# The second pair's q and k are loaded ahead of the first weights, and two loads of weights wait for a word from VectorE

## The chip, the cores and the metric

The kernel runs on one core of a Trainium2 chip, as one program. The metric is the device time of one execution in microseconds (us). The kernel before was timed three times: 749.03 us median (748.67 to 751.96). One more execution was recorded by the hardware profiler and gives all rows below: it took 752.57 us, of which 750.9 us are the span of the trace and the other 1.7 us lie around it.

The engines are called as in the profile: PE is TensorE, DVE VectorE, ACT ScalarE, POOL GpSimd, and SP is SyncE, which does nothing here but issue transfers. Each engine works through its own instructions in order, and so does the queue of transfers that SP issues: an instruction that waits holds up all that stand behind it on that engine.

## The reference

Windowed attention with a linear bias, over 8 batches, 8 heads, 576 positions and a head size of 64, followed by a layer that takes the elementwise maximum of three products:

```
scores = q @ k.T / sqrt(64) + bias              # per batch and head
attn   = softmax(where(0 <= i - j < 128, scores, -1e9))
x      = (attn @ v), heads side by side         # 4608 x 512
h      = max(max(x @ w1, x @ w2), x @ w3)       # 4608 x 768
out    = h @ w_out                              # 4608 x 512
```

## The kernel before, in words

Two heads make a task, four tasks a batch. A task's queries are cut into blocks of 128, and one block of the two heads is a *step*; two tasks share their last half block, so that two tasks make nine steps. Two steps that follow each other are a *turn pair*: they share a set of statistics, and their probabilities are transposed together.

A step runs through four engines. `products` (line 431, PE) multiplies q and k of two steps into PSUM; these are the first users of a task's q and k. `score` (lines 447 to 461, DVE) moves the masked half over the other, adds the bias and takes the row maximum. `exps` (line 473, ACT) takes the exponential and its row sums. `sums_of` (line 479 on ACT, line 480 on DVE) makes the reciprocals of a pair, and `normalise` scales the probabilities with them, on POOL (line 487) or ACT (line 492). `turn` (line 500, PE) transposes the pair, ACT copies it out of PSUM (lines 504, 509, 512), POOL cuts the two triangles (lines 520 and 524), and `mix` (line 545, PE) multiplies with v. Products of a step that holds the last half block of one task and the first block of the next need q and k of both tasks. That happens first in the third pair of steps.

The twelve groups of weights are prepared beside this. `fetch` (line 152) loads one group of 1 MB, in a 64-bit form; `exponents` and `convert` (lines 166, 177, 186 on DVE for the first six groups, lines 170 and 171 on ACT later) make floats of it; `part` (lines 200 and 203) splits these into a high and a low part; lines 327 and 216 write them back to DRAM, as `plain` and `keep`. There are two buffers for raw groups (the tiles `hs`, two buffers under this name): a group can be fetched only when the one two ahead of it is done, its `plain` written included. `preparing` is this sequence for all groups, and each call of `weights(n)` lets it advance by n of its pieces.

What is issued when is set by `events`, a list of steps with times in units of a step, sorted and run at the end of the kernel: `score` of step s at s + 0.04, `exps` at s + 0.3, and so on; `weights` stands in it at 2.06, and from step 5 on at every s + 0.2. A scheduler may still move instructions past each other on an engine, except those marked `keep_in_program_order`, which hold their order among themselves: `score` of the steps below 4, and the transfers and spins that say so. `spin` puts products of zeros on PE between other work.

Ahead of the events stand the first loads, all on SP's queue: q and k of task 0 in two pieces, the first group of weights, q and k of task 1, v of task 0, the second group of weights. `load` and `load_v` are the transfers of a task's q and k and of its v, with two buffers each: the load for task 2 waits until PE is through with task 0.

After the first batch's steps PE starts on the products of the layer (line 767, then line 791), whose left operands are the split weights in `ring`, and from there on it goes through the batches with attention of the next one in between.

Of the kernel before, what the change touches and what calls it, by code (L numbers as in the profile page):

```python
# [8 lines left out]
F32 = mybir.dt.float32  # L9
# [28 lines left out]
def attention_maxout_kernel(  # L38
# [11 lines left out]
    nc = tc.nc  # L50
# [40 lines left out]
    for a in range(2):  # L91
        for d in (slice(0, P),) if a == 0 else (slice(0, D), slice(D, P)):
            nc.gpsimd.affine_select(
                out=prev[d, a], in_=prev[d, a], pattern=[[1, P]], compare_op=ALU.is_gt, fill=0.0,
# [13 lines left out]
    def slopes_t(pair):  # L108
        for h in range(2):
            d = slice(h * D, (h + 1) * D)  # L110
            for j in range(2):
                nc.gpsimd.tensor_scalar(  # L112
                    out=bias_t[d, pair, j], in0=dist[d, 1], scalar1=slope(4 * pair + 2 * h + j), scalar2=None,
                    op0=ALU.mult,
                )

    def slopes(hp):
        for h in (2 * hp, 2 * hp + 1):
            nc.scalar.activation(bias[:, h, :], dist[:, 0], AF.Copy, scale=slope(h))
        nc.gpsimd.affine_select(  # L120
            out=bias0[:, 2 * hp:2 * hp + 2], in_=bias[:, 2 * hp:2 * hp + 2], pattern=[[0, 2], [-1, P]],
            compare_op=ALU.is_ge, fill=-NEG, base=0, channel_multiplier=1,
        )
# [21 lines left out]
    SMALL = DM // 2  # L145

    def raw_tile():
        return hs_p.tile([P, SMALL + 4 * DM], I32, name="hs2", bufs=2)

    def fetch(g):  # L150
        r = raws[g] = raw_tile()
        nc.sync.dma_start(r[:, SMALL:].bitcast(U8)[:, :16 * DM - 3], w_all[g].bitcast(U8)[:, 3:])

    def pieces(g):
# [167 lines left out]
    def preparing():  # L322
        for n, g in enumerate(g_order):
            exponents(g, n < FEW)
            yield
            convert(g, n < FEW)
            nc.sync.dma_start(plain_keep[g], floats(g))
            yield
            for k in range(2):
                while g < 9 and not ahead(g, 1):  # L330
                    yield True
                part(g, k)
                if k == 1 and n + 2 < NG:
                    fetch(g_order[n + 2])
                yield
# [51 lines left out]
    qkt, vt = {}, {}  # L387


    def load(t):  # L390
        b, hp = tasks[t]
        qkt[t] = qk_p.tile([P, 2, S], F32, name="qk")
        for cs in (slice(0, 2 * P), slice(2 * P, S)) if t == 0 else (slice(0, S),):
            nc.sync.dma_start(qkt[t][:, :, cs], qk[b, hp, :, :, cs])

    def load_v(t):
        b, hp = tasks[t]
        vt[t] = v_p.tile([P, NB + 1, P], F32, name="v")
        nc.sync.dma_start(vt[t], v[b, hp])
# [38 lines left out]
    def score(s):  # L438
        t, i = steps[s]
        b, hp = tasks[t]  # L440
        ps, a = banks.pop(s)
        first = tc.keep_in_program_order if s < 4 else lambda x: x
        if i:
            mask = prev[:, i == NB].bitcast(mybir.dt.uint8)
            if a is None:
                for x in ps:
                    first(nc.vector.copy_predicated(x[:, P:2 * P], mask, x[:, :P]))
            else:
                both = scores[:, :, a * 2 * P:(a + 1) * 2 * P]
                first(nc.vector.copy_predicated(  # L450
                    both[:, :, P:], mask.unsqueeze(1).broadcast_to([P, 2, P]), both[:, :, :P],
                ))

        if s % 2 == 0:
            stats[s // 2] = st_p.tile([P, 3, 2, 2], F32, name="st")
        st = stats[s // 2]
        less[s] = []
        for j in range(2):
            x = s_p.tile([P, P], F32, name="s", bufs=3)
            below = bias_t[:, hp // 2, j] if i == NB else (bias if i else bias0)[:, 2 * hp + j, :]  # L460
            first(nc.vector.tensor_tensor_reduce(  # L461
                out=x, in0=ps[j][:, P:2 * P], in1=below,
                scale=-0.125, scalar=3.0e38, op0=ALU.add, op1=ALU.min, accum_out=st[:, 0, s % 2, j:j + 1],
            ))
            less[s].append(x)
# [406 lines left out]
    def at(when, what, *args):  # L872
        events.append((when, len(events), what, args))
# [3 lines left out]
    for s, (t, i) in enumerate(steps):  # L877
        c = s + shift[tasks[t][0]]
        if i == LOAD_I and t + 2 < len(tasks):
            at(c - 0.4, load, t + 2)  # L880
        if i == NB - 1 and t + 1 < len(tasks):
            at(c - 0.4, load_v, t + 1)
        if i == 0 and 0 < t < NP:
            at(c - 1, slopes, t)
            if t % 2 == 0:
                at(c - 1, slopes_t, t // 2)
        at(c + 0.04, score, s)
        at(c + 0.3, exps, s)
        if s % 2 == 0:
            at(c + 0.002, products, s)  # L890
            at(c + DRAIN[0].get(n_steps - s, LAG_T) + 0.003, turn, s)
        else:
            at(c + (0.6 if s == n_steps - 1 else 1.1), sums_of, s)
            at(c + (0.8 if s == n_steps - 1 else 1.5), normalise, s)
# [31 lines left out]
            when += pace if u < 77 * b + 63 else O_PACE  # L926
    for u in range(77 * B, 77 * B + 3):
        at(when, unit, u)
    at(2.06, weights, 1)
    for s in range(5, n_steps + 2):  # L930
        at(s + 0.2, weights, 1.4 if s > 5 else 0.6)
    for s in range(3, n_steps, 2):
# [7 lines left out]
    spin(FIRST_SPIN)  # L940
    load(0)
    nc.scalar.dma_start(dist[:, 2], c_ident)
    fetch(0)
    slopes(0)
    slopes_t(0)
    load(1)
    load_v(0)
    nc.scalar.copy(out=plus, in_=dist[:, 2])
    fetch(1)
    for _, _, what, args in sorted(events, key=lambda e: e[:2]):  # L950
        what(*args)

# [37 lines left out]
```

## Time and profile before

| | us |
|---|---|
| median of three runs | 749.03 |
| profiled execution | 752.57 |
| its span | 750.9 |
| PE busy | 733.9 (98%) |
| DVE busy | 515.2 (69%) |
| ACT busy | 487.2 (65%) |
| POOL busy | 236.4 (31%) |

The busy times are of the whole span. PE is busy for nearly all of it, but part of that in the first 57 us are the spins. What a change at the start is worth is read from the few waits of PE, from the granted clock of PE by stretches, and from the order of the first instructions in time. A row of the timeline gives the start, the duration, the engine, the line, the operation with its tiles, how many instructions are merged in the row, and in brackets the idle time ahead of it with what ended that.

### The profile page before, as it was taken

How to read it: one execution, taken by the hardware profiler on the slowest of the kernel's cores; microseconds unless marked ns; L12 is line 12 of the kernel's file. 1: busy time of each engine (PE TensorE's matmuls, PEld its weight loads, DVE VectorE, ACT ScalarE, POOL GpSimd, SP SyncE). 2: the span in 40 equal slices, each digit the busy share in tenths (PEclk: the TensorE clock that was granted, in tenths of full speed). 3: DMA queues.
4: the chain of work that ended last, by engine and by line, in shares of the span. 5: the costliest groups of instructions: out<-in, count | busy, mean ns of one | idle time of the engine just before them, and what ended most of it. 6: DMA issues, size and time to landing. Idle time of an engine off the chain costs nothing.

```text
span 750.9 us, 19281 instructions
## 1 busy us (share of the span) xinstructions
PE 733.9 (98%) x7209; PEld 674.6 (90%) x7214; DVE 515.2 (69%) x1614; ACT 487.2 (65%) x1603; POOL 236.4 (31%) x451
## 2 busy tenths in 40 slices
PE   7999989999999999999999999999999999999998
PEld 3459988999999999999999999999999999999998
DVE  4888887536659477784778567794777747683673
ACT  5786976766667767676677757776666767552342
POOL 4661224645556123212222123222222122343100
PEclk8999999999999999999999999999999999999999
DMA  7877999759998489855988378864988468899611
GB/s 252 274 282 298 330 340 331 253 187 340 361 349 275 134 279 303 273 181 192 322 294 276 116 266 304 291 213 146 330 289 273 163 228 272 252 291 355 230 61 64
DMA packets 57085, 192.81 MB, mean 257 GB/s; under 512 B 5792, under 2 KB 24480, under 8 KB 50464
## 3 DMA queue, kind: packets, MB, share of 16 engines
q0 software_dynamic: 20304, 108.54, 43.9%
q1 hardware_dynamic: 36400, 82.85, 31.2%
q8 instruction: 57, 0.93, 0.5%
q14 instruction: 36, 0.29, 0.1%
q10 hardware_dynamic: 288, 0.20, 0.1%
HBM read 156.95 MB, written 34.60 MB: 255 GB/s over the span
## 4 chain that ended last, share of the span: by engine, by line
PE 77%; DVE 11%; ACT 7%; DMA 2%; issue 1%; POOL 1%; SPq 0%; DVEq 0%; ACTq 0%; POOLq 0%
PE ps_m L846 46%; PE ps_m L791 16%; PE ps_s L431 5%; PE pt L500 4%; PE ps_x L567 4%; DVE hs L615 2%; DVE hq L733 2%; ACT p L473 2%; DVE t L732 2%; DMA qk<-in_qk 1%; PE ps_x L545 1%; DMA hs<-in_w_all 1%; ACT p L492 1%; DVE t L618 1%; DVE xs L615 1%
## 5 line engine op out<-in xcount | busy, mean ns | idle before, releaser
L846 PE MATMUL ps_m<-xs,ring 128*128 128x288 f32 x2160 | 302.7, 297 | 0.6
L846 PEld LDWEIGHTS ps_m<-xs,ring 128*128 128x128 f32 x2160 | 290.1, 188 | 3.7 <-ACT t L863 3.4
L520 POOL TENSOR_SCALAR_AFFINE_SELECT pp<-pr 128x256 f32<-128x256 f32 x112 | 53.9, 482 | 277.2 <-ACT pr L504 154.0
L473 ACT ACTIVATE p<-s,st 128x128 f32<-128x128 f32 x288 | 114.7, 400 | 20.8 <-DVE st L461 17.2
L863 ACT COPY t<-ps_m 128x288 f32<-128x288 f32 x196 | 76.7, 394 | 71.2 <-PE ps_m L846 69.5
L791 PE MATMUL ps_m<-xs,ring 128*128 128x288 f32 x846 | 118.1, 297 | 2.8 <-DVE hq L808 2.2
L791 PEld LDWEIGHTS ps_m<-xs,ring 128*128 128x128 f32 x846 | 113.3, 188 | 4.1 <-DVE hq L808 2.4
L367 POOL DMA_DIRECT2D ring<-keep x103 | 55.5, 539 | 165.5 <-PE ps_m L846 157.3
L846 PE MATMUL ps_m<-hs,ow 128*128 128x288 f32 x756 | 105.8, 297 | 0.4
L846 PEld LDWEIGHTS ps_m<-hs,ow 128*128 128x128 f32 x756 | 100.9, 188 | 2.6 <-ACT t L863 1.2
L492 ACT ACTIVATE p<-p,st 128x128 f32<-128x128 f32 x252 | 84.6, 393 | 24.1 <-DVE st L480 24.1
L732 DVE TENSOR_TENSOR t<-ps_m,t 128x288 f32<-128x288 f32 x108 | 48.8, 453 | 42.8 <-PE ps_m L846 32.5
L461 DVE CUSTOM_DVE_ANT_0 s<-ps_s,bias 128x128 f32<-128x128 f32 x240 | 60.6, 285 | 9.0 <-POOL bias_t L112 3.4
L431 PE MATMUL ps_s<-qk 64*64 64x192 f32 (+1 forms) x1088 | 62.0, 319 | 3.4 <-DMA qk<-in_qk 2.4
L614 ACT CAST hs<-hq 128x288 fp32r<-128x288 f32 x96 | 40.2, 432 | 30.8 <-DVE hq L733 18.1
L473 ACT ACTIVATION_READ_ACCUMULATOR p<-s,st 128x1 f32 x288 | 55.3, 192 | 0.0
L567 PE MATMUL ps_x<-pp,v 64*64 64x64 f32 (+3 forms) x1456 | 53.4, 274 | 0.1
L567 PEld LDWEIGHTS ps_x<-pp,v 64*64 64x64 f32 x1456 | 41.7, 133 | 10.5 <-issue 8.6
L500 PE MATMUL pt<-plus,p 128*128 128x128 f32 x288 | 48.5, 289 | 2.0 <-POOL p L487 1.3
L524 POOL TENSOR_SCALAR_AFFINE_SELECT pp<-pr 128x256 f32<-128x256 f32 (+1 forms) x112 | 50.0, 447 | 1.1
L733 DVE TENSOR_TENSOR hq<-t,hq 128x288 f32<-128x288 f32 x108 | 48.8, 457 | 2.1
L601 DVE TENSOR_TENSOR xk<-ps_x,xk 128x256 f32<-128x256 f32 (+3 forms) x56 | 25.4, 454 | 36.0 <-ACT xk L600 36.0
(94 smaller groups left out, 942.0 us busy)
## 6 DMA issues: line engine op xcount, KB each, us to landing
ring<-keep POOLq DMA_DIRECT2D x51, 1024.0 KB, 7.4
ring<-keep POOLq DMA_DIRECT2D x61, 768.0 KB, 6.1
qk<-in_qk SPq DMA_DIRECT2D x31, 576.0 KB, 5.3
hs<-in_w_all SPq DMA_DIRECT2D x12, 1023.6 KB, 7.2
v<-in_v SPq DMA_DIRECT2D x32, 320.0 KB, 6.5
outT<-t SPq DMA_DIRECT2D x64, 144.0 KB, 1.8
keep<-ring SPq DMA_DIRECT2D x9, 768.0 KB, 6.5
plain<-hs SPq DMA_DIRECT2D x12, 512.0 KB, 4.0
```

Source lines behind the costliest of these rows:

```text
L367: nc.gpsimd.dma_start(wts[n, a], keep[n % 9][a])
L431: pe(nc.tensor.matmul(ps[j][d:d + D, o:o + k1 - k0], lhsT=qkt[u][j * D:(j + 1) * D, 0, q0:q0 + D], rhs=qkt[u][j * D:(j + 1) * D, 1, k0:k1] ...
L461: first(nc.vector.tensor_tensor_reduce(out=x, in0=ps[j][:, P:2 * P], in1=below, scale=-0.125, scalar=3.0e38, op0=ALU.add, op1=ALU.min, acc ...
L473: nc.scalar.activation(p[:, j], x, AF.Exp, bias=st[:, 0, a, j:j + 1], scale=-1.0, accum_out=st[:, 1, a, j:j + 1])
L492: nc.scalar.activation(p[:, j], p[:, j], AF.Copy, scale=st[:, 2, a, j:j + 1])
L500: pe(nc.tensor.transpose(out=pt[:, a, j], in_=p[:, j], identity=ident))
L567: pe(nc.tensor.matmul(x[j * D:(j + 1) * D, r, o:o + rhs.shape[1]], lhsT=vv[k, i, j * D:(j + 1) * D], rhs=rhs[k], start=start, stop=True, s ...
L732: nc.vector.tensor_tensor(out=s, in0=ps, in1=e, op=ALU.add)
L733: nc.vector.tensor_tensor(out=h, in0=s, in1=h, op=ALU.max)
L791: pe(nc.tensor.matmul(ps, lhsT=lt, rhs=rt, start=n == 0 and not (b == 0 and v < EARLY), stop=n == len(pairs) - 1, skip_group_check=True,))
L846: pe(nc.tensor.matmul(part_of[n, {2: 0, 5: 0, 6: 0, 3: 1}.get(kk, kk)], lhsT=lt, rhs=rt, start=first, stop=i == len(pairs) - 1, skip_group ...
L863: nc.scalar.copy(out=e, in_=ps)
```

## The change

Three things are done.

- `load(1)`, q and k of the second task, is issued ahead of `fetch(0)`, the first group of weights.
- `fetch(0)` is held back: DVE copies one word of task 0's q and k into the buffer of the weights, and the transfer overwrites this word. So it can't be issued before the first piece of q and k has landed and DVE has copied the word.
- `fetch(1)` leaves the first loads and becomes an event at 4.07, where DVE first writes one zero to its buffer. The first piece of the weights' preparation, line 166 for group 0, moves from 2.06 to 4.06, just ahead. `score` of step 4 joins the instructions that keep their program order, so both stand behind that step's scores on DVE.

```
-    def fetch(g):
+    def fetch(g, behind=False):
         r = raws[g] = raw_tile()
+        if behind:
+            tc.keep_in_program_order(nc.vector.memset(r[:, SMALL:SMALL + 1], 0))
+        if g == 0:
+            tc.keep_in_program_order(nc.vector.tensor_copy(out=r[:, SMALL:SMALL + 1].bitcast(F32), in_=qkt[0][:, 0, :1]))
         nc.sync.dma_start(r[:, SMALL:].bitcast(U8)[:, :16 * DM - 3], w_all[g].bitcast(U8)[:, 3:])
...
-        first = tc.keep_in_program_order if s < 4 else lambda x: x
+        first = tc.keep_in_program_order if s < 5 else lambda x: x
...
-    at(2.06, weights, 1)
+    at(4.06, weights, 1)
+    at(4.07, fetch, 1, True)
...
     load(0)
     nc.scalar.dma_start(dist[:, 2], c_ident)
+    load(1)
     fetch(0)
     slopes(0)
     slopes_t(0)
-    load(1)
     load_v(0)
     nc.scalar.copy(out=plus, in_=dist[:, 2])
-    fetch(1)
```

The lines below line 150 move down by four in the kernel after, and by a few more further on (166 becomes 170, 461 becomes 465, 480 becomes 484). Names with a number are single buffers.

The first rows of SP's queue are these before: `qk` are q and k, `hs` the raw weights, and a load of 128x1152 is a whole task.

```order
L394 DMA qk<-in_qk 128x2x256
L394 DMA qk<-in_qk 128x2x320
L152 DMA hs_161<-in_w_all 128x8189
L394 DMA qk<-in_qk 128x1152
L399 DMA v<-in_v 128x640
L152 DMA hs_177<-in_w_all 128x8189
L394 DMA qk<-in_qk 128x1152
```

The same place of SP's queue after:

```order
L398 DMA qk<-in_qk 128x2x256
L398 DMA qk<-in_qk 128x2x320
L398 DMA qk<-in_qk 128x1152
L156 DMA hs_163<-in_w_all 128x8189
L403 DMA v<-in_v 128x640 x2
L398 DMA qk<-in_qk 128x1152
L156 DMA hs_277<-in_w_all 128x8189
```

The load of the second task has moved ahead of the first weights, and the second weights have moved behind the v of task 1 and the q and k of task 2.

On DVE the scores of the second pair of steps, the first piece of the weights (166) and the reciprocals of the first pair (480) stand like this before:

```order
L461 ISA s,st<-ps_m_206,bias 128x128
L461 ISA st 128x1
L166 TENSOR_SCALAR hs_161<-hs_161 128x1024
L480 RECIPROCAL st<-st 128x4
L447 COPY_PREDICATED ps_m_205<-prev,ps_m_205 128x128
```

After, DVE's stretch from the same scores on begins so:

```order
L465 ISA s,st<-ps_m_205,bias 128x128
L465 ISA st 128x1
L484 RECIPROCAL st<-st 128x4
L451 COPY_PREDICATED ps_m_204<-prev,ps_m_204 128x128
L451 COPY_PREDICATED ps_m_205<-prev,ps_m_205 128x128
```

and a few rows further on DVE (`bias_t` marks step 4) it has:

```order
L465 ISA s,st<-ps_s,bias_t 128x128
L465 ISA st 128x1
L170 TENSOR_SCALAR hs_163<-hs_163 128x1024
L153 MEMSET hs_277 128x1
L484 RECIPROCAL st<-st 128x4
```

The first pair's reciprocals no longer stand behind the weights, but the second pair's now do, and the zero that lets group 1 be fetched stands behind the first piece of group 0.

The scheduler's order changes later too. On SP, where the seventh group of weights is written back and the ninth is fetched, it is before:

```order
L327 DMA plain_140<-hs_708 128x1024
L216 DMA keep_0_124<-ring 128x512
L216 DMA keep_1_125<-ring 128x1536
L394 DMA qk<-in_qk 128x1152
L152 DMA hs_860<-in_w_all 128x8189
```

The same place on SP after:

```order
L331 DMA plain_140<-hs_710 128x1024
L220 DMA keep_0_124<-ring 128x512
L398 DMA qk<-in_qk 128x1152
L220 DMA keep_1_125<-ring 128x1536
L156 DMA hs_862<-in_w_all 128x8189
```

The write of 768 KB (`keep_1`) has moved behind the load of q and k, directly ahead of the fetch.

## Rows read from the trace of the kernel before

**Rows 1.** PE's waits above 2 us but the start: total, times, longest.

```profile
PE ps_s L431 <- DMA qk<-in_qk: 2.4, 1, 2.4
PE ps_m L791 <- DVE hq L808: 2.2, 1, 2.2
```

**Rows 2.** Windows of 0.5 and 2 us: length, PE busy, granted clock, DMA share, GB/s.

```profile
10.50:11.00 0.50, 0.00 (x0) 0.59 1.04 435
...
17.50:18.00 0.50, 0.50 (x5) 1.00 0.00 0
...
102.00:104.00 2.00, 0.00 (x0) 1.00 0.67 238
```

**Rows 3.** Timeline of the first 20 us, all engines.

```profile
4.27 1.35 PE L431 MATMUL ps_s<-qk 64*64 64x128 f32 x16
...
9.66 0.41 POOL L120 TENSOR_SCALAR_AFFINE_SELECT bias<-bias 128x256 bf16<-128x256 bf16 x1
9.79 0.83 DVE L166 TENSOR_SCALAR hs<-hs 128x1024 int8<-128x1024 int8 x1 [1.39 <-DMA hs<-in_w_all]
10.54 0.16 DVE L480 RECIPROCAL st<-st 128x4 f32<-128x4 f32 x1
...
10.79 0.61 POOL L487 TENSOR_TENSOR p<-p,st 128x256 f32<-128x256 f32 x1 [0.71 <-DVE st L480]
...
11.26 1.34 PE L431 MATMUL ps_s<-qk 64*64 64x192 f32 x14 [2.41 <-DMA qk<-in_qk]
...
12.53 1.11 PE L500 MATMUL pt<-plus,p 128*128 128x128 f32 x4
...
14.21 0.22 ACT L479 ACTIVATE st<-st 128x4 f32<-128x4 f32 x1
...
15.14 0.62 POOL L487 TENSOR_TENSOR p<-p,st 128x256 f32<-128x256 f32 x1
...
19.34 0.59 ACT L504 COPY pr<-pt 128x512 f32<-128x512 f32 x1 [2.58 <-PE pt L500]
```

**Rows 4.** The page's group for the exponentials on ACT.

```profile
L473 ACT ACTIVATE p<-s,st 128x128 f32<-128x128 f32 x288 | 114.7, 400 | 20.8 <-DVE st L461 17.2
```

**Rows 5.** Timeline from 20 to 30 us, all engines.

```profile
22.10 2.06 POOL L487 TENSOR_TENSOR p<-p,st 128x256 f32<-128x256 f32 x2
...
22.92 0.77 DVE L166 TENSOR_SCALAR hs<-hs 128x1024 int8<-128x1024 int8 x1
...
24.21 0.44 PE L500 MATMUL pt<-plus,p 128*128 128x128 f32 x2 [0.58 <-POOL p L487]
...
25.20 0.18 DVE L480 RECIPROCAL st<-st 128x4 f32<-128x4 f32 x1 [1.09 <-ACT st L479]
...
26.18 1.58 POOL L487 TENSOR_TENSOR p<-p,st 128x256 f32<-128x256 f32 x1
...
28.04 0.30 DVE L447 COPY_PREDICATED ps_m<-prev,ps_m 128x128 f32<-128x128 uint8 x1 [0.75 <-PE ps_m L431]
...
28.33 0.66 PE L500 MATMUL pt<-plus,p 128*128 128x128 f32 x4
```

**Rows 6.** PE's timeline at the first product of the layer.

```profile
57.52 2.67 PE L791 MATMUL ps_m<-xs,ring 128*128 128x288 f32 x18 [0.63 <-DVE xs L615]
```

**Rows 7.** Transfers issued from 3.6 to 4.2 us: size, us to landing.

```profile
hs<-in_w_all SPq DMA_DIRECT2D x1, 1023.6 KB, 10.7
```

**Rows 8.** Transfers issued from 26.4 to 26.8 us.

```profile
hs<-in_w_all SPq DMA_DIRECT2D x1, 1023.6 KB, 5.1
```

**Rows 9.** SP's issues from 62 to 80 us, start and duration.

```profile
66.65 1.28 SPq L216 DMA_DIRECT2D keep<-ring  x2
70.22 0.33 SPq L394 DMA_DIRECT2D qk<-in_qk  x1
```

**Rows 10.** A window of 1 us, columns as in rows 2.

```profile
68.00:69.00 1.00, 1.00 (x10) 1.00 1.02 397
```

**Rows 11.** The chain that ended last, from 0 to 130 us: start, us, what.

```profile
70.65 7.38 DMA hs<-in_w_all
```

## The prediction

> **What bounds the kernel now.** I read first the waits of PE over the whole span [rows 1], then the granted clock in short windows [rows 2], then the first 30 us in order of time [rows 3, 5]. The reader is to see that PE hardly waits: beside the start, which the change leaves alone, two waits are over 2 us. One of them, 2.4 us for q and k of task 1, belongs to the loads that the change reorders. The timeline places it: PE stops at 11.26 - 2.41 = 8.85 us and goes on at 11.26 [rows 3]. The windows show a second cost of it: the granted clock is down to a mean of 0.59 between 10.50 and 11.00, after some 2 us in which PE did nothing, and only from 17.50 on is it 1.00 again [rows 2]; in between PE ran at 1.2 GHz instead of 2.4. The timeline shows a third: DVE stood idle for 1.39 us, to 9.79, waiting for the first weights, and behind line 166 on DVE stood the reciprocals of the first pair (10.54), for which POOL waited 0.71 us [rows 3]. So the first 30 us are bound by a chain of small steps through all engines, not by PE's throughput, and what they lose goes straight into the end: PE starts its layer at 57.52 [rows 6], when the steps let it, and hardly waits from there on.
>
> **The change part by part.** I follow the first pairs of steps, with durations from the rows, and give for each point the time before and after.
>
> *First transposes.* DVE is through with the scores of the second step at 9.79 - 1.39 = 8.40, and line 480 now stands there, so the reciprocals come at about 8.5 instead of 10.54. POOL can't use that at once: it works on bias tables until 9.66 + 0.41 = 10.07 [rows 3]. Its scaling takes 0.61, so it ends at 10.68 and PE transposes from 10.7 instead of 12.53. Q and k of task 1 must be there by 8.85 for this. They now have 576 KB of task 0 and two small tables ahead of them, in place of these and 1 MB of weights; DMA moved about 400 GB/s when full [rows 10], so I put them at 7 to 7.5 us. PE's products then end by 9.6 at the latest (fourteen took 1.34 us at half clock), and PE has a new wait of about 1.1 us, for POOL.
>
> *Clock.* This wait is half the old one, and the clock fell only after some 2 us of nothing. I take it to stay at 1.00. If so, the four transposes take 0.66 as at 28.33 [rows 5] and not 1.11, and with one product that now stands among them they end at 11.5; before they ended at 13.64.
>
> *Second pair.* From the end of the transposes to the end of POOL's scaling of the second pair it took 15.14 + 0.62 - 13.64 = 2.12 us [rows 3], all of it copies on ACT and cuts on POOL, which the clock doesn't touch. So 13.6. Transposes of 0.66 end at 14.3. ACT has, behind line 479 (14.21 before, 0.57 after the transposes, so 12.1 now), six exponentials and scalings of about 0.4 each [rows 4], which ends at 14.5. I put the copy of line 504 at 14.7 instead of 19.34: 4.6 earlier.
>
> *Third pair.* From there to the transposes at 24.21 it took 4.87 us, cuts and scalings on POOL (22.10 to 24.16 the last) that nothing in the change shortens. So 19.6, still 4.6 earlier. DVE has more to do beside this than before: lines 166 and 177 of group 0, which it used to do while it waited anyway, now stand further back. The reciprocals at 25.20 had waited 1.09 us for ACT; in the new order ACT has one exponential and one copy more ahead of line 479 (about 0.65), so I put them at 21.1, 4.1 earlier. At 28.04 DVE had waited 0.75 for PE [rows 5]. With PE 4.6 and DVE 4.1 ahead I take **4.4 us** for this place.
>
> *The held weights.* The copied word costs DVE one tiny instruction at about 4.3, while DVE waits for the first scores anyway; cost nothing, and if that cover were gone a tenth of a us. SP stands still for it until about 4.5, since PE's first products show the first piece of q and k to be there at 4.27 [rows 3], and behind it stand only v of tasks 0 and 1, needed at about 13. Group 0, issued at 4.5, must land by 11.6 (line 166 needs 0.83, and the reciprocals behind it wait for ACT until 12.4). The zero for group 1 follows at about 11.9; before, group 1 was issued at 3.8 and used at 22.92 [rows 5]. With everything 4 us earlier it is due at about 19. One transfer of weights took 5.1 us in a quieter queue [rows 8] and 10.7 with two loads and the other weights ahead [rows 7]. I take 6, near the quieter row, since less than 1 MB is queued ahead of each: 10.5 and 17.9, both in time. At the other end (15.2 and 22.6, later still with the first) the 4.4 are lost.
>
> *Later.* Between 28 and 57 us PE waits for no transfer (the one for q and k is at 11 us, [rows 1]); I carry the 4.4 through. Then the new order on SP counts. The two writes left at 66.65, and the load of q and k at 70.22, when PE let go of a buffer [rows 9]; the fetch behind it lands after 7.38 us and stands in the chain that ended last [rows 11]. Now the second write, 768 KB, leaves behind the load and ahead of the fetch. At 397 GB/s [rows 10] it delays the fetch by up to 1.98 us; part of it is given back, since the old write was still running when the fetch started and since PE reaches the products that free the buffer somewhat sooner. Bounds 0 and 2.0; I take the middle, **1.0 us**. The chain goes from there to PE's wait for line 808 near 102 us [rows 1], so I let it through in full.
>
> The Trainium skill (DMA: Bandwidth & Descriptors, "Queues, rings and completion order") says that each DMA engine takes the descriptors of a queue in ring order. The order of landing bears it out: the first weights end DVE's wait at 9.79, and q and k, issued behind them, end PE's at 11.26 [rows 3]. By that rule alone the whole 768 KB would pass ahead of the fetch, and the sum would be 4.4 - 2.0 = 2.4.
>
> Sum: 4.4 - 1.0 = 3.4 us. The profiled execution would go from 752.57 to 749.2; it lies 3.5 above the median of the runs shown, and I take the same 3.4 from the median: 749.03 - 3.4 = **745.6 us**.
>
> **The rivals.**
> - *The front's gain arrives whole.* If the moved write costs nothing, or the new order on ACT (each pair's exponentials a little earlier against the weights) shortens the wait of 2.2 at 102 us, the gain is 4.4 to 6.6: 742.4 to 744.6. For it: PE's waits there come from one chain that a reorder can relieve. Against it: the rows on DVE ahead of that wait stand nearly as before. Chance 0.25.
> - *POOL is held up by DVE.* Line 487 took 0.62 at 15.14 and 1.58 at 26.18, where DVE ran its long conversion [rows 3, 5]. After, that conversion of group 0 falls next to POOL's scaling of the second pair. Price 1.58 - 0.62 = 1.0 on the chain: gain 2.4, 746.6. The Trainium skill (SBUF — State Buffer, "SBUF: two separate sides") has this as a rule: DVE, with two SBUF inputs or in a two-port mode, and GpSimd share one pair of ports, and whoever starts second is blocked for the whole instruction. The trace agrees with it at 26.18. Chance 0.15.
> - *The clock falls all the same.* PE's short wait could suffice, since the stretch before it is thin too. Then PE's work from 11 to 17 us again takes twice as long, about 2.5 us of the chain: gain 0.9, 748.1. Against it: the wait of 2.2 us near 102 left the clock at 1.00 [rows 2]. Chance 0.12.
> - *Slower: the held weights come late.* DVE waits in order, so a late group 1 stops all scores. It is due at 19 and was used at 22.92; it decides from a landing at 23.3 on, 11.4 us after its issue at 11.9, or earlier if group 0's lateness moves the issue. With 10.7 us for both [rows 7], group 0 lands at 15.2, the zero follows at 16.1 and group 1 lands at 26.8: 26.8 - 22.92 = 3.9 later than before, 752.9. Against it: the 10.7 us had over 2 MB ahead. Chance 0.06.
> - The forecast itself: 0.42, with 744.2 to 747.0 as its own range.
>
> **How the numbers follow.** 0.5%, about what a measurement of this kernel can tell from no change, is 3.75 us. The forecast's 3.4 lies just inside, so its own chance falls on both sides: I give 0.20 of it to faster. With the first rival's 0.25 that is 0.45, and 0.02 from front gains I priced too low: faster 0.47. Same gets the other 0.22 of the forecast, 0.15 and 0.12 less the 0.02, so 0.47. Slower 0.06. The range goes from the first rival's far end, 742.4, over the clock's 748.1 to 749.3, where the held weights eat all of the gain; the fourth rival and what little lies below 742.4 stay outside.
>
> **What would show it.** In the profile after: no wait of PE for q and k, a wait for POOL of about 1 us near 10 us, granted clock 1.00 from 10 to 18 us; line 504 of the second pair at 14.7 and the transposes of the third at 19.6; line 166 of both groups without a wait for the transfer. Line 791's first product 4.4 earlier than the 57.52 of before, and the fetch behind the moved write 1 us longer than 7.38 shows the later term. Wrong would be a wait of DVE for either group of weights over 1 us, a clock of 0.5 anywhere near 12 us, or a lead at line 791 that differs from the lead at 28 us by more than 1 us.

## The result, and the profile after: slower by 0.6 per cent

The kernel after takes 755.70 us, the median of ten runs (753.18 to 757.49), against 750.02 for ten of the kernel before on the same chip: a ratio of 1.0062, 95% interval 1.0046 to 1.0078 (the ratios here and below are those on record for the runs side by side, not the quotients of the two medians). The forecast was 745.6, with 742.4 to 749.3 as its range. The change costs 5.7 us by these medians; a later comparison of the same two kernels gave 754.81 against 751.89 (1.0043, interval 1.0024 to 1.0062), so 3 to 6 us.

| | before | after |
|---|---|---|
| profiled execution, us | 752.57 | 753.23 |
| its span, us | 750.9 | 751.5 |
| its mean granted clock | 0.995 | 0.997 |

The two profiled executions differ by 0.7 us only: that of before is slow for its kernel (752.57 where the ten runs lie between 748.67 and 751.96), that of after fast for its own (753.23 where they lie between 753.18 and 757.49). The experiments begin there.

PE's waits after (total, times, longest) answer to [rows 1]:

```profile
PE pt L504 <- POOL p L491: 5.2, 4, 2.0
...
PE ps_m L795 <- DVE hq L812: 2.2, 1, 2.2
PE ps_s L435 <- DVE st L465: 2.2, 2, 2.0
PE ps_x L549 <- POOL pp L524: 0.9, 1, 0.9
```

The wait for q and k is gone. In its place PE waits four times for GpSimd's scaling, twice for a score of VectorE and once for a cut.

The timeline of the kernel after, from 7 to 26 us, all engines, answers to [rows 3, 5]; line 491 is 487 of before, 504 is 500, 508 is 504, 524 and 528 are 520 and 524, 484 is 480:

```profile
10.70 0.44 PE L504 MATMUL pt<-plus,p 128*128 128x128 f32 x2 [1.99 <-POOL p L491]
10.83 0.69 DVE L170 TENSOR_SCALAR hs<-hs 128x1024 int8<-128x1024 int8 x1 [0.30 <-DMA hs<-in_w_all]
...
15.84 0.59 ACT L508 COPY pr<-pt 128x512 f32<-128x512 f32 x1 [0.61 <-PE pt L504]
...
16.44 0.68 DVE L190 SCALAR_TENSOR_TENSOR hs<-hs 128x512 uint32<-128x512 uint32 x1
16.50 0.90 POOL L524 TENSOR_SCALAR_AFFINE_SELECT pp<-pr 128x256 f32<-128x256 f32 x1 [2.29 <-ACT pr L508]
...
17.90 0.87 POOL L524 TENSOR_SCALAR_AFFINE_SELECT pp<-pr 128x256 f32<-128x256 f32 x1
...
18.73 0.86 POOL L528 TENSOR_SCALAR_AFFINE_SELECT pp<-pr 128x256 f32<-128x256 f32 x1
...
19.57 0.68 DVE L170 TENSOR_SCALAR hs<-hs 128x1024 int8<-128x1024 int8 x1
...
20.78 1.01 PE L504 MATMUL pt<-plus,p 128*128 128x128 f32 x4 [1.69 <-POOL p L491]
...
25.47 0.33 PE L504 MATMUL pt<-plus,p 128*128 128x128 f32 x1
```

The first transposes begin at 10.70, the second pair's copy stands at 15.84 (19.34 before), the third pair's transposes begin at 20.78, their second half at 21.35 (23.19 and 24.21 before), the fourth pair's at 25.47 (28.33 before). Both held weights come in time: line 170 waits 0.30 us for the first and not at all for the second. GpSimd's four cuts of the second pair last from 16.50 to 19.56.

The windows (length, PE busy, granted clock, DMA share, GB/s) after, against [rows 2]:

```profile
10.50:11.00 0.50, 0.30 (x2) 1.00 1.07 426
17.50:18.00 0.50, 0.50 (x4) 1.00 0.04 16
113.00:114.00 1.00, 0.00 (x0) 1.00 1.02 405
115.00:116.00 1.00, 1.00 (x16) 0.63 0.96 397
116.00:117.00 1.00, 1.00 (x9) 0.50 1.10 283
118.00:119.00 1.00, 1.00 (x8) 0.67 0.75 279
```

The clock holds at 1.00 in the front, and falls to 0.50, the 1.2 GHz level, after PE had nothing to do from 113 to 114.9 us. Of the work between 115 and 119 us that costs at most 1.7 us (0.37, 0.50 twice and 0.33 of the four windows; the third is as the second).

Line 791's first product [rows 6], line 795 now, and the fetch of the chain [rows 11] after:

```profile
56.53 1.19 PE L795 MATMUL ps_m<-xs,ring 128*128 128x288 f32 x7
```

```profile
68.71 8.25 DMA hs<-in_w_all
```

The lead over the profiled execution of before is 57.52 - 56.53 = 1.0 us here; behind the wait near 113 us and the fall at 115 us nothing is left.

### The profile page after: what moved, and what is told of

The parts are those of the page before. It is cut to its first block, busy times and chain, and to the rows that moved or that the text cites. A ratio compares the mean times of both kernels' runs of the same rounds, so it can differ in the third digit from the quotient of the medians.

```text
span 751.5 us, 19285 instructions
## 1 busy us (share of the span) xinstructions
PE 732.3 (97%) x7209; PEld 674.7 (90%) x7214; DVE 516.5 (69%) x1616; ACT 487.9 (65%) x1603; POOL 236.7 (31%) x451
## 4 chain that ended last, share of the span: by engine, by line
PE 76%; DVE 13%; ACT 5%; DMA 2%; POOL 2%; issue 1%; SPq 0%; ACTq 0%; DVEq 0%; POOLq 0%
PE ps_m L850 45%; PE ps_m L795 16%; PE ps_s L435 5%; PE pt L504 4%; PE ps_x L571 4%; DVE hs L619 2%; DVE hq L737 2%; DVE t L736 2%; ACT p L477 1%; DMA hs<-in_w_all 1%; DVE t L622 1%; DMA qk<-in_qk 1%; DVE hs L190 1%; ACT p L496 1%; DVE ring L207 1%
## 5 line engine op out<-in xcount | busy, mean ns | idle before, releaser
L504 PEld LDWEIGHTS pt<-plus,p 128*128 128x128 f32 x288 | 30.6, 141 | 26.1 <-issue 13.7
```

The source lines that it names most:

```text
L504: pe(nc.tensor.transpose(out=pt[:, a, j], in_=p[:, j], identity=ident))
```

## The experiments

All times are medians in us, each with the ratio to the kernel before on the same chip and its 95% interval.

| run | median | before | ratio | interval |
|---|---|---|---|---|
| before_again | 752.04 | 751.89 | 0.999 | 0.9971 to 1.0009 |
| after_again | 754.81 | 751.89 | 1.0043 | 1.0024 to 1.0062 |
| load_only | 751.16 | 751.89 | 0.9985 | 0.9963 to 1.0006 |
| no_word | 754.74 | 751.89 | 1.0034 | 1.0019 to 1.0049 |
| holds_early | 751.75 | 751.47 | 1.0005 | 0.9985 to 1.0025 |
| late_only | 751.02 | 751.47 | 1.0006 | 0.9982 to 1.0029 |
| holds_2_6 | 751.53 | 751.47 | 1.0003 | 0.9984 to 1.0022 |
| before_fill | 749.87 | 751.47 | 0.9977 | 0.9960 to 0.9995 |
| order_kept | 755.12 | 751.27 | 1.0056 | 1.0034 to 1.0078 |
| holds_kept | 752.09 | 751.27 | 1.0016 | 0.9993 to 1.0039 |
| before_fill5 | 749.88 | 751.27 | 0.9988 | 0.9971 to 1.0005 |
| after_fill | 756.01 | 751.27 | 1.0063 | 1.0040 to 1.0086 |
| zero_early | 755.77 | 752.11 | 1.0061 | 1.0040 to 1.0083 |
| zero_late | 755.09 | 752.11 | 1.0046 | 1.0026 to 1.0066 |
| late_fill | 748.83 | 752.11 | 0.9963 | 0.9947 to 0.9979 |

**Both kernels once more.** Two theories stood against each other: that the clock falls in new places, and that the new order of instructions loses time at full clock.

> The kernel before, unchanged, so that a second profiled execution and the mean granted clock of each run can be set beside those of the change. Both theories expect 749 to 751 us. Clock theory (the change loses because the granted clock falls at places where it didn't fall before): the runs at 749 us have a mean clock at or above 0.996, higher than most runs of the change (0.993 to 0.998), and the profile shows 1.00 between 113 and 120 us. Order theory (the new order of instructions loses the time at full clock): the mean clocks lie between 0.993 and 0.998 as those of the change do, and the time differs all the same.

> The change, unchanged, for a second profiled execution. Both theories expect 753 to 757.5 us. Clock theory: if this profile is of an execution at 755 us or more, it shows 2 to 4 us more of half clock than the first profile (which had it only between 115 and 119 us), at a place where PE waited for about 2 us just before; the order of instructions and the waits are otherwise those of the first profile. Order theory: the clock is 1.00 at all places but 115 to 119, and the extra time lies in waits.

The profiled execution of before_again took 748.57 us, with a span of 746.9. Its timeline, all engines, and its windows of PE:

```profile
10.85 0.77 PE L431 MATMUL ps_s<-qk 64*64 64x192 f32 x14 [2.52 <-DMA qk<-in_qk]
...
11.55 0.66 PE L500 MATMUL pt<-plus,p 128*128 128x128 f32 x4
...
16.77 0.41 POOL L520 TENSOR_SCALAR_AFFINE_SELECT pp<-pr 128x256 f32<-128x256 f32 x1 [2.32 <-ACT pr L504]
...
18.04 0.85 POOL L524 TENSOR_SCALAR_AFFINE_SELECT pp<-pr 128x256 f32<-128x256 f32 x1
...
19.97 1.01 PE L500 MATMUL pt<-plus,p 128*128 128x128 f32 x4 [0.19 <-POOL p L487]
```

```profile
10.50:11.00 0.50, 0.15 (x4) 1.00 1.11 459
...
102.00:103.00 1.00, 1.00 (x12) 0.50 0.89 362
```

```profile
53.82 1.45 PE L791 MATMUL ps_m<-xs,ring 128*128 128x288 f32 x9 [0.63 <-DVE xs L615]
```

PE waits 2.52 us for q and k, as in the first profile (2.41 [rows 3]), and yet the clock is 1.00 behind it. The third pair's transposes begin at 19.97 and line 791's first product at 53.82, 3.70 ahead of the 57.52 of the first profile [rows 6], with the same instructions in the same order. Of the 3.7 us the first profile has 0.4 from q and k that landed later (11.26 against 10.85), some 2.8 from the half clock of [rows 2] (the transposes at 17.91 stand at 14.69 here, 3.2 apart), and the rest from GpSimd's two scalings ahead of the third pair, 2.06 us [rows 5] against 1.61. All of it is there in some executions and not in others. Against this profile the change has little lead to lose: it is 0.85 ahead at the first transposes (11.55 against 10.70), 0.8 behind at the third pair, 2.7 behind at line 791's first product, and 4.6 at the end (751.5 against 746.9). At most 1.7 of that is the fall at 115 us, and before_again has a fall of the same size of its own, from 101 to 105 us. PE's waits over the whole span sum to 14.2 us in the change and to 10.5 in before_again, 3.7 of the 4.6. The loss is made in the first 124 us: at the transposes that stand at 119.06 here and at 123.52 in the change the distance is 4.5 already.

after_again (754.9 us in its profiled execution) shows two stretches of half clock, from 21.9 to 25 us and, where the first profile had it, from 117 to 121. Both theories miss here: 749 to 751 was expected of before_again, and its median is 752.04; the order theory expected no further half clock in after_again. The mean clock of each run says more. At 0.995 the eleven runs of the change in these two comparisons have a mean of 755.5, and 44 of before, over all later comparisons, 752.5. The difference is 3.0 us at the same recorded clock; so most of the loss isn't in the recorded clock. The recorded clock doesn't make the whole spread of before either: at a mean of 1.000 its 20 runs lie between 748.34 and 753.56.

**One part of the change at a time.** load_only is the kernel before with the load moved:

```diff
+    load(1)
     fetch(0)
...
-    load(1)
```

> The kernel before with one edit: q and k of the second pair are loaded ahead of the first weights; neither fetch is held back and the weights' steps keep their times. If holding back the weights is what costs (later steps of the weights shift the work on VectorE and ScalarE), this run is at 745 to 749 us, at or below the kernel before. If the early load itself moves the rest into a worse order, or into the clock's fall, it is at 753 to 757 as the whole change is. VectorE would wait here for the first weights until about 10.5 us, about 0.7 longer than before.

no_word is the change without the copied word:

```diff
-        if g == 0:
-            tc.keep_in_program_order(nc.vector.tensor_copy(...))
```

> The change without the copied word: the first weights start at once behind q and k of the second pair; the second fetch stays behind the zero. VectorE's order is the same but for that one instruction. Theory that the hold of the first weights matters: q and k of the second pair land later than in the change and PE waits for them again (over 0.5 us), the time moves by more than 2 us. Order and clock theories: no wait for q and k, and 753 to 757 us as in the change, within 1.5.

The early load alone changes nothing that can be measured (751.16 lies between the two ranges that were expected), and the word neither helps nor harms. What is left is the pair of numbers and the second hold. Three kernels take these apart: holds_early has both numbers put back, holds_2_6 a number between, late_only the later number without any hold.

```diff
holds_early, against the change
-    at(4.06, weights, 1)
-    at(4.07, fetch, 1, True)
+    at(2.06, weights, 1)
+    at(2.07, fetch, 1, True)
holds_2_6, against the change
+    at(2.6, weights, 1)
+    at(2.61, fetch, 1, True)
late_only, against load_only
-    at(2.06, weights, 1)
+    at(4.06, weights, 1)
```

> The change with two numbers put back: the first step of the weights stands at 2.06 again and the held second fetch at 2.07, instead of 4.06 and 4.07. The early load and both holds stay. All five engines then have the order of the kernel before, but for the two words that VectorE writes and the order of the loads. Order theory (the change loses 3 us because its later number makes the scheduler place the weights' conversions, and with them scores and exponentials, in a worse order up to 115 us): 750 to 752.5 us, as the kernel before (751.9 over 47 runs) and as the early load alone (751.2). Hold theory (the held transfers are what costs): 754 to 756, as the change. Clock theory (new stretches of idle PE lower the clock): this order has the old stretches, so 750 to 752.5 too, but with the mean clock of the kernel before (0.9965) and not the change's 0.9953.

> The early load, no hold at all, and the first step of the weights at 4.06 instead of 2.06: the number alone. Order theory: this order isn't the change's, but it is reshuffled to the same extent against that of the kernel before (122 rows of PE differ, 93 in the change), so I expect a loss of 1 us or more: 752.5 to 756. Hold theory: 750.5 to 752, as the early load alone.

> The change with the first step of the weights at 2.6 (and the held second fetch at 2.61): VectorE has the first reciprocals ahead of line 166 of the first weights, as in the change, but all that comes later keeps the order of the kernel before (VectorE differs in 4 rows, the copied word and the zero among them, ScalarE in 4). Order theory: the part of the change that I counted on is here, 0.85 us at the first transposes (10.70 against 11.55), without the reshuffle: 749 to 751.5 us, 0.5 to 2 below the kernel before on the same chip. Hold theory: 754 to 756.

All three are at the level of before. So the held transfers cost nothing that can be measured by themselves, and two of the order theory's expectations miss: the number alone, which reshuffles as many rows, loses nothing, and the reciprocals ahead of the weights (holds_2_6) gain nothing. In holds_2_6 VectorE waits 1.8 us for the first weights behind them, so what the early reciprocals are worth without that wait isn't shown. Of these kernels only the change, with the late number and the second hold together, is slow.

**Order or transfer.** The zero is pinned to its place in the program, so it acts twice: it holds the fetch, and it fixes VectorE's order around it. order_kept leaves the fetch free and keeps the pinned zero, written to another buffer; holds_kept was meant to keep every hold and only takes the pin from the zero.

```diff
order_kept, against the change
-    at(4.07, fetch, 1, True)
+    at(4.07, lambda: tc.keep_in_program_order(nc.vector.memset(warm, 0.0)))
...
+    fetch(1)
holds_kept, against the change
-            tc.keep_in_program_order(nc.vector.memset(r[:, SMALL:SMALL + 1], 0))
+            nc.vector.memset(r[:, SMALL:SMALL + 1], 0)
```

> The change with its order on all engines (PE, ScalarE and GpSimd row for row the same), but without the hold of the second group of weights: that fetch starts at the beginning, as before, and the zero that stands for it in the order goes to a small buffer of its own. Order theory (the change loses because the pinned zero together with the later first step of the weights gives the scheduler another order): 754 to 756 us, as the change (755.1). Hold theory (the second group's late transfer costs, each of the two edits alone being harmless): 750.5 to 752.5, as the kernel before.

> The change with all its loads and both holds as they are, but the zero that holds the second fetch isn't pinned to its place in the program. That alone makes the order on PE, ScalarE and GpSimd that of the kernel with the early load and the step at 4.06 alone (751.0 us), row for row. Order theory: 750.5 to 752.5. Hold theory: 754 to 756.

The order is enough: 755.12 with the order of the change and without the second hold, where the second weights leave at 5.18 us instead of 11.57. holds_kept, on the same chip, has 752.09, but it isn't the kernel that its expectation describes. Without the pin the zero moved ahead to 4.24 us (11.47 in the change), and the second weights leave at 5.74; the hold went with the order. That a late second fetch costs nothing by itself is shown by holds_early, where it leaves at 11.24 in the order of the kernel before. SP's fetch of the second weights in the change, in order_kept, in holds_kept and in holds_early:

```profile
11.57 0.33 SPq L156 DMA_DIRECT2D hs<-in_w_all  x1
```

```profile
5.18 0.56 SPq L154 DMA_DIRECT2D hs<-in_w_all  x1
```

```profile
5.74 0.35 SPq L156 DMA_DIRECT2D hs<-in_w_all  x1
```

```profile
11.24 0.33 SPq L156 DMA_DIRECT2D hs<-in_w_all  x1
```

**Where in the order.** zero_early puts only the held fetch back to 2.07, zero_late only the first step of the weights to 2.06.

```diff
zero_early, against the change
-    at(4.07, fetch, 1, True)
+    at(2.07, fetch, 1, True)
zero_late, against the change
-    at(4.06, weights, 1)
+    at(2.06, weights, 1)
```

> The change with the held second fetch at 2.07 instead of 4.07; the first step of the weights stays at 4.06. VectorE's order is the change's in its first 134 rows, up to about 45 us, but for two groups of one or two rows at row 37; behind it the order is another, nearly the one of the next run. If the front of the change's order loses the time: 753.5 to 756 us, and in the profile GpSimd's four cuts of the second pair (16.50 to 19.56 in the change, 3.06 us, against 2.10 in the kernel before) are as long as in the change. If the loss is made behind 57 us: 750.5 to 752.5, or as the next run.

> The change with the first step of the weights back at 2.06; the held second fetch stays at 4.07. VectorE's first 89 rows and PE's first 57, up to about 22 us, are those of the kernel before; behind it the order is nearly that of zero_early. If the front loses the time: 750.5 to 752.5 us, at least 1.5 below zero_early, and GpSimd's cuts of the second pair take about 2.1 us. If the loss is made behind 22 us by an order that the pinned zero at 4.07 brings: 753.5 to 756, as zero_early.

Both are slow, zero_late with the front of the kernel before and its first step of the weights at 2.06. So neither the front nor that number is what these two share with the change, but the pinned zero in a place where the scheduler makes another order behind it. GpSimd's cuts, 3.06 us in the change and 2.10 in before_again (16.77 to 18.87), leave the change 0.8 us behind at the third pair, but they take 2.28 us in zero_early (where the scaling ahead of them took 1.61) and 2.10 in zero_late, which are as slow. The waits of PE from 28 to 112 us show the rest, first of before_again, then of the change (total, times, longest; the change's waits of 2.2 for line 812 and of 0.9 for a cut, shown above, belong here too):

```profile
PE ps_m L791 <- DVE hq L808: 2.0, 1, 2.0
PE ps_m L791 <- DVE xs L615: 0.6, 1, 0.6
...
PE ps_x L545 <- POOL pp L520: 0.4, 2, 0.2
```

```profile
PE pt L504 <- POOL p L491: 1.6, 2, 1.3
...
PE ps_m L795 <- ACT hq L809: 0.5, 1, 0.5
```

The new waits are for GpSimd's scaling and cuts and for a copy, 1.6 + 0.9 + 0.5 against 0.4 for GpSimd and 0.6 for the layer's operands (line 615): 2.0 us more. The 0.5 stands at 88 us; all waits between 28 and 57 us sum to 3.2 in the change and 2.0 in before_again. So of the 2.7 us at line 791's first product 0.8 is the front's and 1.2 are these; for the rest the traces give no wait. One place has changed in both slow kernels. VectorE's rows of before_again near 48 us, of the change near 50 and of zero_late near 56:

```profile
46.41 1.50 DVE L203 TENSOR_TENSOR ow<-hs,ow 128x512 fp32r<-128x512 f32 x2 [0.87 <-ACT ow L200]
47.86 0.29 DVE L461 CUSTOM_DVE_ANT_0 s<-ps_s,bias 128x128 f32<-128x128 f32 x1
```

```profile
49.59 0.29 DVE L465 CUSTOM_DVE_ANT_0 s<-ps_s,bias 128x128 f32<-128x128 f32 x1 [1.33 <-PE ps_s L435]
...
49.81 1.65 DVE L207 TENSOR_TENSOR ow<-hs,ow 128x512 fp32r<-128x512 f32 x2
51.38 0.28 DVE L465 CUSTOM_DVE_ANT_0 s<-ps_s,bias 128x128 f32<-128x128 f32 x1
...
51.70 0.43 DVE L454 COPY_PREDICATED ps_s<-prev,ps_s 128x256 f32<-128x256 uint8 x1
```

```profile
55.35 0.29 DVE L465 CUSTOM_DVE_ANT_0 s<-ps_s,bias 128x128 f32<-128x128 f32 x1 [1.34 <-POOL pp L524]
...
55.78 1.58 DVE L207 TENSOR_TENSOR ow<-hs,ow 128x512 fp32r<-128x512 f32 x2
57.28 0.42 DVE L454 COPY_PREDICATED ps_s<-prev,ps_s 128x256 f32<-128x256 uint8 x1
```

Line 203 (207 after), 1.5 to 1.65 us that split one group of weights, stands ahead of the last step pair's scores (line 461) in the kernel before. In the change it stands between the two scores, in zero_late behind both and ahead of the mask (line 454) of the step that follows, so that what needs those instructions comes later by as much; in late_fill and holds_early it is ahead of the scores, as in before_again. That this place carries the loss is read from the traces and was not tried by itself; which of the reshuffled rows between 22 and 112 us costs how much stays open.

**The clock.** before_fill gives PE ten matmuls of the idle tile where it waits for q and k, before_fill5 five, and after_fill six in the change at the wait near 113 us:

```diff
before_fill (before_fill5: 5), against the kernel before
+    at(4.0015, spin, 10)
after_fill, against the change
+    at(34 + shift[...] + 0.0015, spin, 6)
```

> The kernel before with ten more matmuls of the idle tile on PE ahead of the fifth step's products, about 2.1 us of work that fills the wait for q and k of the second pair from 8.3 to 10.4 us; the order of the other engines is unchanged. Clock theory for the spread of the kernel before (its profiled execution at 752.6 had half clock from 10.6 to 17.5 us after this wait and was 3.7 us behind from 25 us on; the one at 748.6 had the same wait of 2.5 us, no fall there, and no other difference): with the wait filled no execution falls there, the runs lie at 748 to 751 and the median is 1 to 2 us lower. If the fall isn't tied to this wait, the median stays within 0.7 us and the profile may show half clock between 10 and 18 us again.

> The kernel before with five filling matmuls ahead of the fifth step's products instead of ten. With ten, each took 0.43 us in the profiled execution, they ended near 13 us and the products of the fifth step began at 13.30 instead of 10.85; still the median was 1.6 us below the kernel before. Clock theory: five of them end at about 10.5, where q and k land; no fall near 12 us in most executions, and what ten lost is back: 747.5 to 749.5 us. If only a longer stretch of work keeps the clock up, half clock between 10 and 18 us shows again and the time is 750 to 752.

> The change with six filling matmuls on PE ahead of the products of the second batch's last but one step, where PE waited 1.95 us for VectorE near 113 us in the first profile and where the granted clock fell right after it (115 to 119 us; in the second profile 117 to 121). The order of the other engines is the same up to there, and differs in some 20 rows of VectorE right behind. Clock theory: no half clock between 113 and 122 us, and 1 to 1.7 us less than the change: 753.3 to 754.2. Order theory alone: the loss is made in the order before 113 us, so the time is still above 753; if the clock there plays no part, 754.5 to 756.

before_fill is faster, by 0.05 to 0.4 per cent, and its twelve runs lie between 748.61 and 751.46 where before has 748.53 to 754.33. None of the twelve has a mean clock of 0.995 or less; of before's runs in the later comparisons 57 of 119 have. PE there, and in before_fill5:

```profile
8.37 4.79 PE L375 MATMUL pt<-hs 128*128 128x512 bf16 x13
13.30 0.77 PE L431 MATMUL ps_s<-qk 64*64 64x192 f32 x16
```

```profile
7.39 2.33 PE L375 MATMUL pt<-hs 128*128 128x512 bf16 x9
9.65 0.54 PE L431 MATMUL ps_s<-qk 64*64 64x192 f32 x2
12.25 0.77 PE L431 MATMUL ps_s<-qk 64*64 64x192 f32 x14 [2.06 <-DMA qk<-in_qk]
```

The ten were too many: the fifth step's products begin at 13.30 instead of 10.85, and what the clock gave is partly spent. The five ended near 9.7 in an execution whose q and k landed at 12.25: 2.06 us of waiting were left and half clock followed (0.50 between 14 and 15 us). The expectation of 747.5 to 749.5 was missed, and the run can't be told from before. after_fill missed too: its clock is 1.00 from 113 to 122 us, but its profiled execution has half clock at 105 to 108 instead, and it is no faster than the change.

late_fill puts the fill where the other, harmless order, that of late_only, had half clock:

```diff
late_fill, against late_only
+    at(8.0015, spin, 4)
```

> The early load and the step at 4.06, no hold, and four filling matmuls on PE ahead of the products of the ninth step, near 18 us, behind which PE waits 0.95 and 0.58 us for GpSimd and the granted clock fell at 21 us in two profiles of this order (half clock for 7 us, some 3.5 us of the chain). VectorE's order is that of late_only (751.0). Clock theory: no half clock between 20 and 28 us in the profile, median 749 to 750.3, below the kernel before. If the fall comes all the same, 750.5 to 752.

Windows of PE in late_only and in late_fill, and PE's timeline around the fill:

```profile
22.00:23.00 1.00, 1.00 (x8) 0.50 1.02 424
```

```profile
22.00:23.00 1.00, 1.00 (x7) 1.00 1.01 416
```

```profile
18.68 1.04 PE L375 MATMUL pt<-hs 128*128 128x512 bf16 x4
...
20.02 0.44 PE L500 MATMUL pt<-plus,p 128*128 128x128 f32 x2
```

748.83 us: faster than before by 0.2 to 0.5 per cent, better than was expected, and some 6 us below the change. None of its twelve runs has a mean clock of 0.995 or less; five of late_only's have. But the clock isn't all of it: at a mean of 0.998 or more, eleven runs of late_fill have a mean of 748.9 and four of late_only 750.8. The fill also changed ScalarE's order, which the expectation doesn't mention. ScalarE near 20 us, first in late_only, then in late_fill:

```profile
21.39 0.37 ACT L512 COPY pr<-pt 128x256 f32<-128x256 f32 x1 [2.58 <-PE pt L500]
```

```profile
19.25 0.40 ACT L473 ACTIVATE p<-s,st 128x128 f32<-128x128 f32 x1 [0.43 <-DVE st L461]
...
21.41 0.37 ACT L512 COPY pr<-pt 128x256 f32<-128x256 f32 x1 [1.27 <-PE pt L500]
```

Two exponentials now run where ScalarE had stood idle. How much of the gain is the clock's, how much these exponentials' and how much the early load's was not taken apart; before_fill has 0.9977 without the early load, and the two intervals overlap.

## Why the prediction was wrong

Two steps failed. One counted the delay of a single execution as the front's gain; without that delay there was little to gain. The other put the new order behind the front at nothing, and the loss was made there.

- *"So the first 30 us are bound by a chain of small steps through all engines, not by PE's throughput, and what they lose goes straight into the end."* Right for the profile that it read, and it is where the first error came in. Most of the 4.4 that I took as the front's gain was the delay of that one execution, 3.7 us against before_again, of which the half clock from 10.5 to 17.5 us made some 2.8. I noted that this execution "lies 3.5 above the median" and took the gain from the median all the same, though an execution without the fall has little there to gain. The change was 0.85 ahead of before_again at the first transposes and 0.8 behind at the third pair. This is the first step that failed.
- *First transposes at 10.7, bound by GpSimd.* Right to 0.05. PE's wait was put at 1.1 and was 1.99, since its products ended at 8.7 and not at 9.6.
- *Clock 1.00 from 10 to 18.* Right in both profiles of the change, by chance: no_word, in the same order, has half clock between 12 and 16 us behind a wait of 1.70 us for GpSimd, where the two profiles of the change had waits of 1.99 and 1.19 and no fall. The rival that the clock falls all the same had a chance of 0.12, as if one execution stood for all.
- *Second and third pair at 14.7 and 19.6.* 15.84, and 21.35 for the second half of the third pair's transposes, which is the place meant (24.21 before; the first half stands at 23.19 there and at 20.78 after). The first transposes ended at 12.08 and not at 11.5, since the two products among them took 0.6 us; the 2.12 us from there to the end of the second pair's scaling came out (14.21). Then PE took ps_x products ahead of the transposes (15.14). The rival on GpSimd didn't come true where it was put, since that scaling took 0.62 us; it came true at its price one step later: the four cuts took 3.06 against 2.10 us, 1.0 more, beside lines 190 (16.44) and 207 on VectorE, which read two inputs from SBUF. The rule in the Trainium skill (SBUF — State Buffer, "SBUF: two separate sides") on the ports that both share agrees with these rows: a cut takes 0.41 us alone and 0.86 to 0.90 where one of these lines had just begun.
- *Held weights in time.* Right: 0.30 us of waiting and none, and holds_early at the level of before. The rival that made them late was the only one on the slower side, and the change is slower for another reason.
- *"I carry the 4.4 through."* Wrong, and the second step that failed: the forecast looked for transfers that PE waits for between 28 and 57 us, found none, and put the new order there at nothing. By the sign that the prediction named itself, the lead over the first profile was 2.9 us at the fourth pair (28.33 against 25.47) and 1.0 at 57.52. Against before_again the change falls from 0.8 behind at the third pair to 2.7 behind at line 791's first product and 4.5 near 119 us. order_kept shows that the order alone makes the loss, and zero_late that the order behind 22 us is enough; which of its rows cost how much stays open.
- *The moved write, 1.0 us.* The fetch took 8.25 instead of 7.38, 0.9 more, but this isn't shown to be the write's: with the write where it was the fetch took 8.81 in holds_early, and with it moved 7.06 in no_word. So the agreement may be luck, and PE's wait for line 808, to which the chain was to lead, is 2.2 us as before.

## What to carry to other kernels

One profile is one draw: before a stretch of half clock is counted as a gain, look whether a second execution has it, and compare the profile's own time with the spread of its kernel. A pinned instruction, even a zero of one word, can make a scheduler rearrange a hundred microseconds on all engines; compare the orders, not the edit. Taking the pin away is no remedy by itself: here the zero then ran 7 us earlier, and the hold was gone. So look in each run whether the instruction and the transfer stand where they were meant to. Where PE waits in a thin stretch, a few idle matmuls gained 0.2 per cent (before_fill); from the early data alone no gain could be measured (load_only).

## What the runs showed that was not expected

- The same wait has two outcomes. 2.41 us of nothing on PE were followed by half clock for 7 us, 2.52 us in the same place of another execution by none, and waits of 0.95 and 0.58 us near 20 us (late_only) again by 7 us of it. The Trainium skill (TensorE: Matmul & The Clock Gate, "What's actually happening") says that the window in which the chip looks at PE doesn't start with the kernel; the runs agree in so far as the same instructions fell in one execution and not in the next.
- What a fall costs depends on what PE waits for behind it. The one at 10.5 to 17.5 us cost some 2.8 us to the end. The one at 101 to 105 us in before_again cost PE 1.5 us (its lead over the first profile went from 3.97 at 100.17 to 2.45 at 104.85), and at 111.02 the lead was 4.00 again: the first profile had waited there instead.
- A granted clock of 1.00 isn't always the rate. Among the thirteen idle matmuls of before_fill the first eight start mostly 0.43 us apart, and from 11.9 us on the last five start 0.22 apart, all in windows that the profile shows at 1.00. The other profiles have the same two distances at 1.00 and change from one to the other earlier: near 6 us in the change and in before_again, near 7 in the first profile of before. So the mean clock of a run leaves out a slow start, and it can't tell runs apart that differ in this.
